# A decode block whose 2560-byte output is stored by two four-row transfers from two engines, in place of one eight-row transfer

## The chip, the cores and the metric

The kernel runs on one core of a Trainium2 chip. The core has a matrix engine (TensorE, PE in the profile), three engines for elementwise work (VectorE or DVE, ScalarE or ACT, GpSimd or POOL), a sequencer without arithmetic that issues transfers (SyncE, SP), and 16 DMA engines that move data between HBM and the on-chip memories. Each engine runs its own list of instructions; they meet through semaphores. The metric is the device time of one execution in microseconds; before the change it is 187.03 us, the median of three runs (186.99 to 187.13).

## The reference

One decode step of a block with adaptive layer norm, for a batch of two rows of 640 numbers in bf16:

```python
mod = (_silu(c) @ w_mod).reshape(c.shape[0], 6, 1, -1)
sa, ca, ga, sb, cb, gb = (mod[:, 0].copy(), ...)
h = _layernorm(x, axis=-1) * (1 + ca) + sa
x = x + ga * _A_ref(h, A_k_cache, A_v_cache, A_wq, A_wo)
h = _layernorm(x, axis=-1) * (1 + cb) + sb
x = x + gb * _B_ref(h, B_w_gate, B_w_up, B_w_down)
return x
```

`_A_ref` is attention with 32 heads of 192 numbers over the last 1024 positions of the two caches, and `_B_ref` is a feed-forward part with 1536 hidden numbers and a gelu gate. The result is 2 x 1 x 640 numbers, 2560 bytes.

## The kernel before, in words

Some 77 MB of caches and weights stream in from HBM, in transfers that SyncE issues in a fixed order: the modulation weights, the two small inputs, the query weights, four K tiles, five V tiles, the output projection, and last the gate, up and down weights of the feed-forward part. The large tiles share a ring of four slots and the space of the query weights, so SyncE waits for an earlier tile's last reader before it issues the load of the next tile.

The rows of the batch are not kept as two long rows. A row of 640 numbers is folded into `NJ = 4` pieces of 160, and piece j of batch row b lies on partition 32 j + 16 b of a 128 x 160 tile. So the eight pieces sit on partitions 0, 16, 32, ... 112 (`rows_of`, L277), and in HBM they are reached by a view of two outer dimensions, four pieces by two batch rows (`dram_rows`, L280). The inputs `c` and `x` come in by this pair of views (L328, L329), and the output leaves by it (L680).

The scores are made on VectorE (products at L465) and summed by TensorE and VectorE (L476, L483); after the softmax the values are summed on TensorE (L523). After the output projection (L628) the second layer norm, the gate and up products (L646), gelu (L653), and the down product (L669) follow each other closely, each with its weights landing shortly ahead. The last two elementwise operations, on VectorE, multiply the down product by the modulation (L676) and add the residual into the tile `sc` (L678).

A small scheduler of the kernel's own (`_Sched`, L28) keeps one list of operations for each engine, in the order in which the program names them. `S.op` adds a computation, `S.dma` a transfer with a semaphore of its own; both work out from the named reads and writes which operations must come first, and `emit` (L79) writes the lists out with a wait ahead of an instruction whose semaphore has not been waited for yet (L93). A transfer's wait is usually folded into the transfer's own instruction at L274. The output transfer is the last entry of SyncE's list; it waits for L678. After it SyncE waits until the transfer has landed (L683), and nothing else stands on any engine. ScalarE's list ends with gelu (L653).

Of the kernel before, what the change touches and what calls it, by code (L numbers as in the profile page):

```python
# [103 lines left out]
def bass_adaLN_cond__sliding_block_cached__geglu_ffn__decode_kernel(  # L104
# [15 lines left out]
    P = 128  # L120
# [5 lines left out]
    SQ = 32  # L126
    NJ = P // SQ
    BS = SQ // 2
# [43 lines left out]
    with es:  # L172
        S = _Sched(nc, es)
# [48 lines left out]
        sc = sb("sc", [P, DN], BF16)  # L222
# [36 lines left out]
        def bank(k):  # L259
            return ("bank", k)  # L260
# [7 lines left out]
        sem_wu = [S.sem("d_wu%d" % i) for i in range(len(WU_SPLIT))]  # L268
        sem_wd = [S.sem("d_wd%d" % i) for i in range(len(WD_SPLIT))]
        sem_ring = [S.sem("d_ring%d" % i) for i in range(4)]  # L270
        sem_out = S.sem("d_out")

        def k_dma(dst, src):
            return lambda e: e.dma_start(dst, src)  # L274


        def rows_of(tile):  # L277
            return tile[0:P:BS, :]

        def dram_rows(v):  # L280
            return v.rearrange("b (j n) -> j b n", j=NJ)
# [8 lines left out]
             reads=[("S", 0, 0, 0), ("S", 0, 0, 1), ("S", 0, 1, 0), ("S", 0, 1, 1)], writes=["ident_f"], name="ident_f")  # L290
        S.op("pool", lambda e: e.tensor_copy(out=ident_b[:, :], in_=ident_f[:, :]),
             reads=["ident_f"], writes=["ident_b"], name="ident_b")
# [3 lines left out]
             reads=["ident_f"], writes=["G32"], name="G32")  # L296
        S.op("dve", lambda e: e.tensor_reduce(out=M32[:, :], in_=ident_f[:, :].rearrange("p (h t) -> p h t", t=QP), axis=AX.X, op=ALU.add),
             reads=["ident_f"], writes=["M32"], name="M32")
# [3 lines left out]
             reads=["G32"], writes=["Bsel"], name="Bsel")  # L302
# [3 lines left out]
             reads=["M32"], writes=["DS"], name="DS")  # L306


        for b in range(2):
            S.op("dve", (lambda b: lambda e: e.tensor_copy(  # L310
                out=SEL[:, b, :, BS * b:P:SQ], in_=G32[:, :].rearrange("p (j m) -> p m j", m=HM)))(b),
                reads=["G32"], writes=["SEL"], name="SEL%d" % b)
        for b in range(2):
            for m in range(HM):
                S.op("dve", (lambda b, m: lambda e: e.tensor_copy(
                    out=Qsel[:, b, m, :].rearrange("p (a m t) -> p a m t", a=NJ, m=HM)[:, :, m, :],
                    in_=ident_f[:, BS * b:P:SQ].unsqueeze(2).broadcast_to([P, NJ, QP])))(b, m),
                    reads=["ident_f"], writes=["Qsel"], name="Qsel%d%d" % (b, m))
# [277 lines left out]
        for i, nt in enumerate(OT_SPLIT):  # L596
            S.op("dve", (lambda t0, nt: lambda e: e.transpose(oT[:, t0:t0 + nt, :], oc.rearrange("p (q k) -> p k q", k=NT)[:, t0:t0 + nt, :]))(t0, nt),
                 reads=[("oc", c) for c in range(NQC)], writes=[("oT", t) for t in range(t0, t0 + nt)], name="oT%d" % i)
# [24 lines left out]
        for i, (ta, tb) in enumerate(wo_of):  # L623
            def f(e, ta=ta, tb=tb):
# [10 lines left out]
             reads=[bank(BK_M), ("modC", 0)], writes=[("lnt", 0)], name="ga_attn")  # L635
        S.op("dve", lambda e: e.tensor_tensor(out=X2[:, 0, :], in0=lnt[:, 0, :], in1=X2[:, 0, :], op=ALU.add),
             reads=[("lnt", 0)], writes=[("X2", 0)], name="x1")
# [3 lines left out]
        def ffn_gu(bk, wv, key, name, ka, kb):  # L641
            def f(e):
# [11 lines left out]
             reads=[bank(BK_G[0])], writes=["gl"], name="gelu")  # L654
        k0 = 0
        for ci, nk in enumerate(WU_SPLIT):
# [4 lines left out]
             reads=[bank(BK_G[1]), "gl"], writes=["aC"], name="geglu")  # L661
        to_contraction(aT[:, :, :], aC[:, :], FT, ["aC"], ["aT"], "aT")
        f0 = 0
        for ci, nf in enumerate(WD_SPLIT):
            def f(e, f0=f0, nf=nf):
# [11 lines left out]
             reads=[bank(BK_C), ("modC", 1)], writes=[("lnt", 1)], name="gb_y")  # L677
        S.op("dve", lambda e: e.tensor_tensor(out=sc[:, :], in0=lnt[:, 1, :], in1=X2[:, 0, :], op=ALU.add),  # L678
             reads=[("lnt", 1), ("X2", 0)], writes=["sc"], name="outC")
        S.dma("sp", k_dma(dram_rows(out[:, 0, :]), rows_of(sc)), sem_out, reads=["sc"], name="st_out")  # L680

        S.emit("sp", nc.sync)
        nc.sync.wait_ge(sem_out, 16)  # L683
        S.emit("pool", nc.gpsimd)
        S.emit("act", nc.scalar)
        S.emit("dve", nc.vector)
# [29 lines left out]
```

## Time and profile before

| what | value |
|---|---|
| median of the runs | 187.03 us (186.99 to 187.13) |
| span of the profiled execution, from its first to its last instruction | 185.7 us |
| mean granted TensorE clock | 0.915 |
| TensorE matmul / VectorE / ScalarE busy | 63% / 57% / 7% of the span |
| read from HBM | 76.88 MB, 414 GB/s over the span |
| issue of the output transfer on SyncE | starts at 183.93 us, lasts 0.635 us |
| SyncE's wait for it to land (L683) | 1.1 us |

The profile gives for the profiled execution its span only; the run times stand 1.3 us above it (187.03 against 185.7), which is what lies around the first and the last instruction. In the lines of the profile a number with L is a line of the kernel, SPq and ACTq are the lists of instructions that SyncE and ScalarE step through, and DMA_DIRECT2D is the instruction that issues a transfer: its duration is the time that the issuing engine spends on it, not the time in which the bytes move. A share such as 57% is an average over stages with different limits; for the change at hand only the last few microseconds matter.

### The profile page before, as it was taken

Reading aid. Unit: us, or ns where it says so; the run is one execution under the profiler, and the core shown is the slowest. Engines: PE = TensorE matmul, PEld = TensorE weight load, DVE = VectorE, ACT = ScalarE, POOL = GpSimd, SP = SyncE. Lnnn points to the kernel's source line nnn. Section 1 sums busy time; section 2 is a strip of 40 time slices with the busy share of each in tenths; the row PEclk is TensorE's granted clock in tenths of the full one; section 3 lists DMA queues with packets and bytes.
Section 4 is the critical chain, followed back from the end, with each engine's and each line's share of the span. In section 5 each row is a group of like instructions: output and inputs, shape, how many; then the busy total and the mean of one; then the engine's idle time right before and its main releaser. Section 6 shows DMA issues by size and latency. Waiting matters only on the chain.

```text
span 185.7 us, 2254 instructions
## 1 busy us (share of the span) xinstructions
PE 117.2 (63%) x1014; PEld 60.8 (33%) x1014; DVE 106.6 (57%) x114; ACT 13.9 (7%) x24; POOL 4.9 (3%) x12
## 2 busy tenths in 40 slices
PE   0004500871079899988999885349928977299844
PEld 0001200440024334433344342226614654265422
DVE  6801600020598999999999993294556714803331
ACT  2001400013000000000000000200010004100400
POOL 8200000000000000000000000000000000000000
PEclk9999999998559999999999999558996999859999
DMA  7999998898999989899999989899999999999991
GB/s 248 414 437 477 463 463 389 371 491 371 487 413 434 468 381 459 381 487 402 455 424 434 459 381 466 381 487 413 395 434 424 424 435 424 413 408 435 422 392 50
DMA packets 2925, 77.02 MB, mean 415 GB/s; under 512 B 356, under 2 KB 356, under 8 KB 868
## 3 DMA queue, kind: packets, MB, share of 16 engines
q1 hardware_dynamic: 2916, 76.88, 96.7%
q8 instruction: 8, 0.13, 0.3%
q14 instruction: 1, 0.01, 0.0%
HBM read 76.88 MB, written 0.00 MB: 414 GB/s over the span
## 4 chain that ended last, share of the span: by engine, by line
DMA 43%; DVE 36%; PE 16%; SPq 1%; ACT 1%; issue 1%; POOL 1%; DVEq 0%; POOLq 0%
DMA ring<-in_A_k_cache_dram 24%; DVE ring L465 19%; DMA ring<-in_B_w_down_dram 18%; PE ps L523 10%; DVE r L465 7%; DVE Sg L483 5%; PE ps L476 4%; DVE Em L511 2%; SPq L274 1%; ACT E_sb L502 1%; PE ps L504 1%; PE ps L498 1%; DVE On L540 0%; ACT On L536 0%; PE ps L491 0%
## 5 line engine op out<-in xcount | busy, mean ns | idle before, releaser
L465 DVE TENSOR_TENSOR ring<-ring,qbc 128x6144 bf16<-128x6144 bf16 x12 | 40.1, 3351 | 8.4 <-DMA ring<-in_A_k_cache_dram 8.4
L476 PE MATMUL ps<-ring,ident_b 128*128 128x512 bf16 x144 | 34.7, 393 | 13.0 <-DVE ring L465 13.0
L454 PE MATMUL ps<-qbc,ident_b 128*128 128x384 bf16 x120 | 24.7, 339 | 0.7 <-ACT qbc L432 0.7
L523 PE MATMUL ps<-ring,Em 128*64 128x384 bf16 x192 | 19.6, 371 | 7.8 <-DVE Em L511 6.6
L476 PEld LDWEIGHTS ps<-ring,ident_b 128*128 128x128 bf16 x144 | 13.6, 100 | 32.7 <-DVE ring L465 17.2
L511 DVE TENSOR_TENSOR Em<-E_sb,M32b 128x2048 bf16<-128x2048 bf16 x8 | 18.1, 2288 | 5.5 <-PE ps L523 5.5
L523 PEld LDWEIGHTS ps<-ring,Em 128*64 128x64 bf16 x192 | 12.4, 125 | 14.6 <-DVE Em L511 7.3
L454 PEld LDWEIGHTS ps<-qbc,ident_b 128*128 128x128 bf16 x120 | 11.6, 101 | 10.9 <-issue 2.8
L401 PE MATMUL ps<-ring,scT 128*32 128x480 bf16 x40 | 4.4, 601 | 16.0 <-DVE scT L358 16.0
L465 DVE TENSOR_TENSOR r<-r,qbc 128x6144 bf16<-128x6144 bf16 x4 | 13.4, 3352 | 0.0
L483 DVE TENSOR_REDUCE Sg<-ps 128x32 f32<-128x512 f32 x16 | 11.0, 687 | 3.4 <-PE ps L476 3.4
L424 PE MATMUL ps<-r,hT 128*32 128x384 bf16 x80 | 5.8, 475 | 10.7 <-DMA r<-in_A_wq_dram 10.7
L476 PE MATMUL ps<-r,ident_b 128*128 128x512 bf16 x48 | 11.1, 380 | 1.8 <-DVE r L465 1.8
L434 DVE CAST aux<-ps 128x384 bf16<-128x384 f32 x4 | 2.0, 553 | 16.6 <-PE ps L424 15.7
L628 PE MATMUL ps<-r,aux 128*32 128x160 bf16 x192 | 5.1, 271 | 4.4 <-DMA r<-in_A_wo_dram 2.6
L424 PEld LDWEIGHTS ps<-r,hT 128*32 128x32 bf16 x80 | 3.2, 135 | 13.8 <-issue 11.6
L476 PEld LDWEIGHTS ps<-r,ident_b 128*128 128x128 bf16 x48 | 4.4, 98 | 8.1 <-DVE r L465 3.4
L401 PEld LDWEIGHTS ps<-ring,scT 128*32 128x32 bf16 x40 | 1.2, 132 | 17.5 <-DVE scT L358 16.0
L540 DVE TENSOR_SCALAR On<-ps,rden 32x192 bf16<-32x192 f32 x4 | 1.7, 418 | 8.9 <-ACT On L536 8.9
L502 ACT ACTIVATE E_sb<-Sg,nb 128x256 bf16<-128x256 f32 x2 | 1.0, 507 | 75.6 <-DVE nb L501 75.6
L628 PEld LDWEIGHTS ps<-r,aux 128*32 128x32 bf16 x192 | 4.3, 114 | 5.8 <-DMA r<-in_A_wo_dram 3.6
L523 PE MATMUL ps<-r,Em 128*64 128x384 bf16 x64 | 5.4, 327 | 0.0
(73 smaller groups left out, 65.6 us busy)
## 6 DMA issues: line engine op xcount, KB each, us to landing
ring<-in_A_k_cache_dram SPq DMA_DIRECT2D x3, 6144.0 KB, 40.3
ring<-in_A_v_cache_dram SPq DMA_DIRECT2D x2, 6144.0 KB, 23.3
r<-in_A_wq_dram SPq DMA_DIRECT2D x1, 7680.0 KB, 30.7
r<-in_A_k_cache_dram SPq DMA_DIRECT2D x1, 6144.0 KB, 38.4
r<-in_A_v_cache_dram SPq DMA_DIRECT2D x1, 6144.0 KB, 23.3
ring<-in_A_v_cache_dram SPq DMA_DIRECT2D x2, 3072.0 KB, 17.6
r<-in_A_wo_dram SPq DMA_DIRECT2D x2, 2560.0 KB, 23.7
ring<-in_w_mod_dram SPq DMA_DIRECT2D x1, 4800.0 KB, 14.2
```

Of the source, the lines that this page charges most:

```text
L274: return lambda e: e.dma_start(dst, src)
L401: last = e.matmul(ps[SQ * j:SQ * j + SQ, bk, 0:3 * DN].rearrange("p (i n) -> p i n", i=3), lhsT=scT[:, k, :], rhs=wm_v[:, k, 3 * part * D: ...
L424: last = e.matmul(ps[SQ * j:SQ * j + SQ, BK_H + c, 0:QC], lhsT=hT[:, k, :], rhs=wq_v[:, k, RN * j + QC * c:RN * j + QC * (c + 1)], start=( ...
L434: S.op("dve", lambda e: e.tensor_copy(out=dst, in_=src), reads=reads, writes=writes, name=name)
L454: last = e.matmul(ps[:, bk, 0:2 * Dh], lhsT=ident_b[:, :], rhs=qbc[:, :, :].rearrange("p b d -> p (b d)"), start=True, stop=True)
L465: S.op("dve", lambda e: e.tensor_tensor(out=tile_v(ks)[:, hf * JH:(hf + 1) * JH, :], in0=tile_v(ks)[:, hf * JH:(hf + 1) * JH, :], in1=qbc[ ...
L476: last = e.matmul(o_ap, lhsT=ident_b[:, :], rhs=tile_v(ks)[:, hf * JH:(hf + 1) * JH, ci * GC:(ci + 1) * GC], start=(ci == 0), stop=(ci == ...
L483: S.op("dve", lambda e: e.tensor_reduce(out=S_sb[:, b, a:a + JH], in_=ps[:, hf, 0:JH * GC].rearrange("p (j c) -> p j c", j=JH), axis=AX.X, ...
L502: S.op("act", lambda e: e.activation(out=E_sb[:, b, :], in_=S_sb[:, b, :], func=ACTF.Exp, scale=SCALE, bias=nb[:, 0:1], accum_out=esum[:, ...
L511: S.op("dve", lambda e: e.tensor_tensor(out=Em[:, t % 2, :, :], in0=E_sb[:, b, J * t:J * (t + 1)].unsqueeze(2).broadcast_to([P, J, H]), in ...
L523: last = e.matmul(ps[r:r + 2 * H, BK_O, 0:ON], lhsT=Em[:, t % 2, 2 * jp:2 * jp + 2, :].rearrange("p j c -> p (j c)"), rhs=tile_v(vs)[:, 2 ...
L628: last = e.matmul(ps[SQ * j:SQ * j + SQ, BK_M, 0:DN], lhsT=oT[:, t, :], rhs=wo_v[:, t, DN * j:DN * j + DN], start=(t == 0), stop=(t == NT ...
```

## The change

The one store of eight rows becomes two stores of four rows. Batch row 0 (partitions 0, 32, 64, 96 of `sc`) is issued by SyncE, batch row 1 (partitions 16, 48, 80, 112) by ScalarE. Each has a semaphore of its own, both wait for L678, and SyncE waits for the two semaphores at the end, one after the other. The view in HBM of each store has one outer dimension of four pieces that follow each other without a gap, where the view before had two. In the order of instructions, SyncE's list keeps its length with the last transfer of the new form; ScalarE's list grows by one transfer at its end; TensorE's, VectorE's and GpSimd's lists are the same.

```diff
-        sem_out = S.sem("d_out")
+        sem_out = [S.sem("d_out%d" % b) for b in range(2)]
...
-        S.dma("sp", k_dma(dram_rows(out[:, 0, :]), rows_of(sc)), sem_out, reads=["sc"], name="st_out")
+        for b, eng in enumerate(("sp", "act")):
+            S.dma(eng, k_dma(out[b, 0, :].rearrange("(j n) -> j n", j=NJ), sc[BS * b:P:SQ, :]), sem_out[b], reads=["sc"], name="st_out%d" % b)

         S.emit("sp", nc.sync)
-        nc.sync.wait_ge(sem_out, 16)
+        for s_out in sem_out:
+            nc.sync.wait_ge(s_out, 16)
```

## The prediction

> **What bounds the kernel now.** I read the chain that ended last first: for 185.7 us it goes through loads, VectorE's products and TensorE's sums, and the change touches none of these. So only the stretch behind the last sum matters, and I read it in the timeline, from the last matmul to the end:
>
> ```profile
> 182.85 0.32 PE L669 MATMUL ps<-ring,aux 128*32 128x160 bf16 x8
> 183.22 0.32 DVE L676 TENSOR_TENSOR lnt<-ps,modC 128x160 f32<-128x160 f32 x1 [2.48 <-PE ps L669]
> 183.58 0.32 DVE L678 TENSOR_TENSOR sc<-lnt,X 128x160 bf16<-128x160 f32 x1
> 183.93 0.64 SPq L274 DMA_DIRECT2D out_dram<-sc  x1
> ```
>
> The columns are start, duration, engine, line. VectorE finishes the output tile just ahead of 183.93, SyncE then spends 0.64 us on issuing the store, to 184.57. What follows is in SyncE's own list of waits:
>
> ```profile
> SPq L274 <- DVE sc L678: 32.7, 1, 32.7
> SPq L683 <- DMA out_dram<-sc: 1.1, 1, 1.1
> ```
>
> SyncE had been waiting 32.7 us for the tile, so it starts the issue at once; and after the issue it waits 1.1 us for the landing. 183.93 + 0.64 + 1.1 = 185.67, the end of the span. Nothing else is on the chip in that time, as the table of stretches shows, cut at the end of the issue:
>
> ```profile
> 184.57:185.19 0.62, 0.00 (x0) 0.00 (x0) 0.00 (x0) 0.00 (x0) 0.00 (x0) 0.80 0.00 0
> 185.19:185.31 0.12, 0.00 (x0) 0.00 (x0) 0.00 (x0) 0.00 (x0) 0.00 (x0) 0.50 0.10 21
> 185.31:185.67 0.36, 0.00 (x0) 0.00 (x0) 0.00 (x0) 0.00 (x0) 0.00 (x0) 0.50 0.00 0
> ```
>
> After the stretch and its length come the five engines' busy time, the clock, the DMA engines' busy share and GB/s. For 0.62 us after the issue no byte moves, the eight rows move within 0.12 us at a share of 0.10, and 0.36 us later the landing is seen. So the tail of 1.74 us is 0.64 issue, 0.62 until the first packet, 0.12 of packets, 0.36 until SyncE goes on. The issue depends most visibly on the form of the transfer; here are SyncE's issues by form, with the least, median and greatest ns:
>
> ```profile
> L274 SPq DMA_DIRECT2D ring<-in_A_v_cache_dram x4: 535/535/535, 82.6 to 130.6; - x4
> L274 SPq DMA_DIRECT2D r<-in_A_wo_dram x4: 343/432/432, 135.8 to 137.2; - x4
> ...
> L274 SPq DMA_DIRECT2D ring<-in_w_mod_dram x1: 373/373/373, 0.8 to 0.8; - x1
> L274 SPq DMA_DIRECT2D cc<-in_c_dram x1: 692/692/692, 1.2 to 1.2; - x1
> L274 SPq DMA_DIRECT2D xc<-in_A_x_dram x1: 547/547/547, 2.0 to 2.0; - x1
> ...
> L274 SPq DMA_DIRECT2D ring<-in_B_w_gate_dram x1: 328/328/328, 147.1 to 147.1; - x1
> L274 SPq DMA_DIRECT2D ring<-in_B_w_up_dram x1: 434/434/434, 147.5 to 147.5; - x1
> L274 SPq DMA_DIRECT2D out_dram<-sc x1: 635/635/635, 183.9 to 183.9; - x1
> ```
>
> The cache tiles have a view with two outer dimensions in HBM (heads by position groups) and cost 535 when SyncE comes out of a wait. The weights have one outer dimension: 328 to 343 out of a wait (the gate weights, the first of the four output projection parts), 432 to 434 when another issue stands right ahead (the other parts, the up weights). The eight-row transfers cost 547 to 692.
>
> **The change part by part.** The sum is made on the profiled execution, whose span of 185.67 us is all that the profile gives of it; 1.3 us lie around that up to the median of 187.03, and I take these as unchanged and apply the difference to the median.
>
> *The store's form, on SyncE.* Removed: one issue of two outer dimensions, 635. Added: one of one outer dimension, four rows. No row shows that form at four rows. Going from two outer dimensions to one is worth 535 - 335 = 200 ns among issues out of a wait, so I take 635 - 200 = 435. The ends are 328, the cheapest issue in the trace, and 635, no gain. That would end SyncE's issue at 183.93 + 0.435 = 184.37, 0.20 us earlier.
>
> *The second store, on ScalarE.* Added: one issue on an engine that issues no transfer before. Its work is done at 175.6 us (gelu starts at 175.14 and lasts 0.49), so it stands waiting for L678 as SyncE does and starts at 183.94; nothing is queued behind it on ScalarE. The trace shows no ScalarE issue, so its price is bounded by SyncE's rows: 328 at the least, at the most 692 for the dearest small issue, or more if it has to queue behind SyncE's. I take 435 as for SyncE, and because both start together I add what an issue pays right behind another, 433 - 328 = 0.105: 0.54 us, to 184.48, against 184.57 before. That is 0.09 us less. This later one of the two sets the end.
>
> *The flight.* 0.62 to the first packet, 0.12, 0.36: taken as before for each store. The rows are eight in all either way, and at a share of 0.10 the 16 DMA engines have room, so two stores side by side cost nothing here; at the worst the second store's packets come after the first's, +0.12 at most, and half the rows for each could take as much as half of 0.12 off.
> The Trainium skill (DMA: Bandwidth & Descriptors, Rules for kernel authors) speaks against the change: two transfers to disjoint partition halves run on the same DMA engines and serialize, so one transfer should be used. By that rule the +0.12 would be paid and the sum would be 187.08; the trace of before holds one store alone and cannot show it.
>
> *The second wait of SyncE, and the new semaphore.* The wait at L683 is one instruction of 17 ns in the trace; a second one behind it adds 0.02 when both transfers have landed, and nothing is queued behind it but the end. I take 0.02; the bounds are 0 and 0.04. ScalarE now ends at 184.48 where it ended at 175.6; whatever follows on it is covered by SyncE, which waits until about 185.6, so it costs nothing while that issue ends before that.
>
> Sum: -0.09 + 0.02 = -0.07 us, 187.03 - 0.07 = 186.96, which I round to 186.95.
>
> **The rivals.** A measurement of this kernel can tell about 0.2% from no change, 0.37 us: below 186.66 or above 187.40.
>
> *Cheaper all along (faster).* Both issues at 328 with no queueing: -0.31 + 0.02, 186.74. To count as faster, another 0.08 must come off the flight, as it would if the 0.62 us between the issue and the first packet were also longer for two outer dimensions than for one: at 0.5 instead of 0.62 the time is 186.62. For it speaks that the 635 is the dearest of all issues out of a wait; against it that no row of an idle queue shows the flight of another form.
>
> *The form saves nothing (same).* Four rows or eight, one dimension or two, 635 each and side by side: 187.03 + 0.02 = 187.05, or the ScalarE issue 0.105 longer, 187.16. The two small loads speak for it, 547 and 692 with the same views: a spread of 145 with no form to explain it.
>
> *One after the other (slower).* If the two issues cannot run at the same time, the second starts when the first is done. At the reduced price the second ends 0.435 + 0.475 (the spacing of two issues of the weights, 147.46 to 147.94) = 0.91 after the start, 0.275 later than before's 0.635: 187.32, still within 0.2%. At the unreduced price it ends at 1.27: +0.635 + 0.02, 187.69. The same time results if ScalarE's first issue alone takes about 1.25 us. It decides from about 1.0 us on: 0.635 + 0.37. For it speaks that an issue behind another is dearer by 0.105 on one engine; against it that 0.105 is far less than a whole issue.
> The Trainium skill (Perfetto Trace Analysis, DMA Instruction — HWDGE) says that the block that generates descriptors is shared by the two issuing sequencers and locked for exclusive use, with the lock wait inside the profiled duration. By that rule one of the two issues would show as longer by up to the other's length; no row of before has two issuers, so only the price between 0.105 and a whole issue is open.
>
> **How the numbers follow.** The sum with its small queueing cost: 0.37, at 186.95, from 186.80 to 187.10. The form saves nothing: 0.10. One after the other at the reduced price: 0.10. One after the other at the full price, or a dear first issue on ScalarE: 0.23. Cheaper all along: 0.20, of which 0.17 below 186.66 and 0.03 between that and 186.74. The rest of the first three cases' spread puts 0.03 more above 187.40. So faster 0.17, same 0.57, slower 0.26. The range reaches down to 186.60 (cheap issues and a flight of 0.5), and up to 187.46: the reduced price in series, 187.32, and the 145 by which the two small loads differ, for a first issue on ScalarE. About 0.04 is left out below and 0.15 above, mostly the full price in series.
>
> **What would show it.** In the profile of after, SyncE's issue should be about 0.44 and ScalarE's about 0.54 us, both starting within 0.02 of each other behind L678; the first packets some 0.6 us after the issue, a DMA share still near 0.1, and SyncE's waits ending about 1.1 us after ScalarE's issue ended. Everything before 183.9 should be as it was. An issue on ScalarE over 1.0 us, or one that starts its packets only after SyncE's have landed, makes the prediction wrong upwards; a stretch without packets shorter than 0.5 us makes it wrong downwards. A change in the loads' stretch would mean that something moved which I took to be untouched.

## The result and the profile after

The changed kernel takes 187.41 us (median of 21 runs, 187.12 to 187.75) against 187.04 us before; the ratio is 1.0018, with a 95% interval of 1.0011 to 1.0024. By that ratio it is 0.34 us slower (0.21 to 0.45), where the prediction had 0.07 faster. Run a second time beside other kernels it came out at 1.0015 (1.0007 to 1.0024). The time lies inside the range; the direction was wrong.

The timeline of the changed kernel's end, with the columns of before:

```profile
182.97 0.32 PE L669 MATMUL ps<-ring,aux 128*32 128x160 bf16 x8
183.35 0.33 DVE L676 TENSOR_TENSOR lnt<-ps,modC 128x160 f32<-128x160 f32 x1 [2.48 <-PE ps L669]
183.71 0.33 DVE L678 TENSOR_TENSOR sc<-lnt,X 128x160 bf16<-128x160 f32 x1
184.06 0.59 SPq L274 DMA_DIRECT2D out_dram<-sc  x1
184.06 1.33 ACTq L274 DMA_DIRECT2D out_dram<-sc  x1
```

Both issues start at 184.06. SyncE's takes 0.59, not the predicted 0.44; ScalarE's takes 1.335 (1.33 in the line above), not 0.54. Where the time goes is clearer in the table of stretches (stretch, length, the engines' busy time, clock, the DMA engines' busy share, GB/s), which I cut at the packets of the two stores:

```profile
184.06:185.29 1.23, 0.00 (x0) 0.00 (x0) 0.00 (x0) 0.00 (x0) 0.00 (x0) 1.00 0.00 0
185.29:185.38 0.09, 0.00 (x0) 0.00 (x0) 0.00 (x0) 0.00 (x0) 0.00 (x0) 1.00 0.08 14
185.38:185.57 0.19, 0.00 (x0) 0.00 (x0) 0.00 (x0) 0.00 (x0) 0.00 (x0) 1.00 0.00 0
185.57:185.66 0.09, 0.00 (x0) 0.00 (x0) 0.00 (x0) 0.00 (x0) 0.00 (x0) 1.00 0.08 14
185.66:186.02 0.36, 0.00 (x0) 0.00 (x0) 0.00 (x0) 0.00 (x0) 0.00 (x0) 1.00 0.00 0
```

SyncE's four rows move 1.23 us after the common start (the packets in the trace: from 185.296), then nothing for 0.19 us, then ScalarE's four rows (from 185.572), 0.28 us behind. The last 0.36 us are as before. So the tail, from the start of the issue to the end of the span, grew from 1.74 to 1.96 us: +0.22. The profiled span is 186.0 us instead of 185.7; the other 0.13 us lie ahead of 184.06, in a stretch that the change does not touch and in which profiles of these kernels differ by more (the first store behind the output tile began between 183.87 and 184.72 us in the runs below). I therefore read the experiments by their tails, and use the times as a check.

SyncE's own waits after the change:

```profile
SPq L274 <- DVE sc L678: 32.5, 1, 32.5
SPq L685 <- DMA out_dram<-sc: 1.3, 1, 1.3
```

The wait for the landing is 1.3 where it was 1.1, although the issue ahead of it is shorter.

### The profile page after: what moved, and what is told of

Read it like the earlier page. It is cut to its first block, busy times and chain, and to the rows that moved or that the text cites. A ratio compares the mean times of both kernels' runs of the same rounds, so it can differ in the third digit from the quotient of the medians.

```text
span 186.0 us, 2255 instructions
## 1 busy us (share of the span) xinstructions
PE 116.6 (63%) x1014; PEld 60.5 (33%) x1014; DVE 106.6 (57%) x114; ACT 13.9 (7%) x24; POOL 4.9 (3%) x12
## 4 chain that ended last, share of the span: by engine, by line
DMA 42%; DVE 36%; PE 17%; SPq 1%; ACT 1%; issue 1%; POOL 1%; DVEq 0%; POOLq 0%
DMA ring<-in_A_k_cache_dram 24%; DVE ring L465 19%; DMA ring<-in_B_w_down_dram 18%; PE ps L523 11%; DVE r L465 7%; DVE Sg L483 5%; PE ps L476 4%; DVE Em L511 2%; SPq L274 1%; ACT E_sb L502 1%; PE ps L504 1%; PE ps L498 1%; DVE On L540 0%; ACT On L536 0%; PE ps L491 0%
## 5 line engine op out<-in xcount | busy, mean ns | idle before, releaser
L476 PE MATMUL ps<-ring,ident_b 128*128 128x512 bf16 x144 | 35.5, 400 | 13.9 <-DVE ring L465 13.9
L454 PE MATMUL ps<-qbc,ident_b 128*128 128x384 bf16 x120 | 23.9, 330 | 0.7 <-ACT qbc L432 0.7
L424 PE MATMUL ps<-r,hT 128*32 128x384 bf16 x80 | 5.0, 422 | 11.0 <-DMA r<-in_A_wq_dram 11.0
```

What stands on the lines that cost most here:

```text
L424: last = e.matmul(ps[SQ * j:SQ * j + SQ, BK_H + c, 0:QC], lhsT=hT[:, k, :], rhs=wq_v[:, k, RN * j + QC * c:RN * j + QC * (c + 1)], start=( ...
L454: last = e.matmul(ps[:, bk, 0:2 * Dh], lhsT=ident_b[:, :], rhs=qbc[:, :, :].rearrange("p b d -> p (b d)"), start=True, stop=True)
L476: last = e.matmul(o_ap, lhsT=ident_b[:, :], rhs=tile_v(ks)[:, hf * JH:(hf + 1) * JH, ci * GC:(ci + 1) * GC], start=(ci == 0), stop=(ci == ...
```

## The experiments

Three theories stood at first. *First issue*: a program's first transfer on ScalarE pays a one-time price. *Queueing*: ScalarE's issue waits for SyncE's. *The engine*: ScalarE always takes 1.3 us for an issue. Below, "start to packet" is the time from the start of a store's issue to its first packet in the trace. In the kernel before it is 1.27 us (183.93 to 185.20). The diffs show the lines that an experiment is about; "..." stands for changes left out, which are the declarations of tiles and semaphores, the wait at the end, and lines that the text names.

**Both stores on SyncE.**

```diff
-        for b, eng in enumerate(("sp", "act")):
+        for b, eng in enumerate(("sp", "sp")):
```

> The two four-row stores are both issued by SyncE, one behind the other; ScalarE issues nothing. Theory 'first issue' (a program's first transfer on ScalarE pays a one-time 0.7 us), theory 'queueing' (ScalarE waits for SyncE's issue) and theory 'the engine' (each issue on ScalarE takes about 1.3 us) agree here on the first issue, 0.59 us as in the changed kernel, if ScalarE's issue beside it did not lengthen it. The second should take 0.43 to 0.6, so that it ends 1.1 to 1.25 us after the start against 0.64 before: 187.5 to 187.65 us. If it ends at or below 187.2, the time is not set by the end of the issue.

Measured: 187.58 us, ratio 1.0031 (1.0020 to 1.0042). The issues take 0.594 and 0.560 us, starting 0.64 apart; each store's first packet stands 1.23 and 1.20 us after its own start, and the tail is 2.29 us, +0.55. The split alone, without ScalarE, costs one issue. With ScalarE it cost 0.22, so the second engine does save something against two stores in one list, but nothing against one store.

**The one store on ScalarE.**

```diff
-        S.dma("sp", k_dma(dram_rows(out[:, 0, :]), rows_of(sc)), sem_out, reads=["sc"], name="st_out")
+        S.dma("act", k_dma(dram_rows(out[:, 0, :]), rows_of(sc)), sem_out, reads=["sc"], name="st_out")
```

> The kernel before with its one store of eight rows issued by ScalarE in place of SyncE. 'First issue' and 'the engine': ScalarE's issue takes 1.3 to 1.4 us with nothing beside it, and the tail from the issue's start to the end of the span is about 1.94 us as in the changed kernel against 1.74 before: 187.2 to 187.4 us. 'Queueing': 0.64 us and 187.0 us.

Measured: 187.05 us, ratio 1.0000 (0.9991 to 1.0009). The issue in the timeline of this kernel, and the stretches behind its start:

```profile
184.72 1.11 ACTq L274 DMA_DIRECT2D out_dram<-sc  x1
```

```profile
184.72:185.98 1.26, 0.00 (x0) 0.00 (x0) 0.00 (x0) 0.00 (x0) 0.00 (x0) 1.00 0.00 0
185.98:186.09 0.11, 0.00 (x0) 0.00 (x0) 0.00 (x0) 0.00 (x0) 0.00 (x0) 1.00 0.11 23
186.09:186.45 0.36, 0.00 (x0) 0.00 (x0) 0.00 (x0) 0.00 (x0) 0.00 (x0) 0.89 0.00 0
```

None of the theories had this. The issue is long without any company (against *queueing*: 1.11 us where SyncE took 0.635), and yet the first packet stands 1.27 us after the start, as from SyncE, the tail is 1.74 us and the time is that of before. (The profiled execution of this kernel is the slowest of its ten, 187.71 us; its excess lies ahead of 184.72.) The extra length of this issue is not on the path: its first packet comes 0.17 us after its end, where SyncE's came 0.63 after the end of a 0.635 us issue.

**ScalarE's store as its second transfer.**

```diff
-        S.dma("sp", k_dma(rows_of(xc), dram_rows(A_x[:, 0, :])), sem_x, writes=["xc"], name="ld_x")
+        S.dma("act", k_dma(rows_of(xc), dram_rows(A_x[:, 0, :])), sem_x, writes=["xc"], name="ld_x")
```

> The changed kernel, with the small load of x at the start issued by ScalarE, so that its store is its second transfer. 'First issue': the load takes about 1.3 us on ScalarE, hidden under the loads, and the store's issue falls to 0.55 to 0.7 us; time 186.95 to 187.1. 'Queueing' and 'the engine': the store's issue stays at 1.3 us, time 187.3 to 187.45.

Measured: 187.19 us, ratio 1.0008 (0.9998 to 1.0017). The load takes ScalarE 1.132 us at the start, the store only 0.563, so the long issue is a matter of the first transfer. But the tail is 1.91 us, +0.17; the time alone would not tell this kernel from before. Now ScalarE's packets come first, 1.21 after the start, and SyncE's are the late ones, 1.48 after theirs. *First issue* is right about the instruction and wrong about the tail.

**Four rows on SyncE, alone.**

```diff
-        sem_out = [S.sem("d_out%d" % b) for b in range(2)]
+        sem_out = [S.sem("d_out0")]
...
-        for b, eng in enumerate(("sp", "act")):
+        for b, eng in enumerate(("sp",)):
```

> SyncE alone stores batch row 0 in the new four-row form; batch row 1 is not stored. It prices the form by itself. If the form is worth the 0.2 us of the prediction, the issue is 0.44 us and the time 186.85. If the 0.592 us of the changed kernel is the form's own price, the issue is 0.59 and the time 186.95 to 187.05: the 0.2 us were wrong whatever ScalarE does. All three theories on ScalarE say the same here, except that 'queueing' with both sides affected would give 0.44.

Measured: 186.99 us, ratio 0.9997 (0.9988 to 1.0006); issue 0.589 us, start to packet 1.23, tail 1.67. The four-row form by itself saves 0.05 of the issue, 0.04 of the way to the first packet and 0.07 of the tail, not 0.2.

From here on the theory was *sharing*: a store's first packet comes about 1.23 us after the start of its issue whatever the issue's length, and of two stores issued together the second is held up by about 0.26 us more. The runs bear out the second half; the first half does not hold, as the next section shows.

**The second store 8 us ahead.** (In the runs of this kind "st_out1" reads the tile of the input x and stands in place of ScalarE's store at the end; SyncE keeps its four-row store.)

```diff
              reads=[bank(BK_G[0])], writes=["gl"], name="gelu")
+        S.dma("act", k_dma(out[1, 0, :].rearrange("(j n) -> j n", j=NJ), xc[BS:P:SQ, :]), sem_out[1], reads=["xc"], name="st_out1")
...
```

> The changed kernel, but batch row 1's store takes its data from the input x, not from the result, and is issued by ScalarE right behind gelu at 175.6 us, 8 us ahead of SyncE's. Both transfers are kept, their coincidence is gone. Theory 'sharing' (each store needs about 1.23 us from the start of its issue to its first packet, and when both are issued together the second is held up by a further 0.26 in something that both issuers share; the length of the issue does not count): SyncE's store as when alone, first packet 1.23 after its start, tail 1.65 us, 186.95 to 187.05. If the changed kernel's loss comes from something that a second transfer costs at any time (the end of the program, another queue), the time stays at 187.3 to 187.45.

Measured: 186.92 us, ratio 0.9993 (0.9984 to 1.0003); ScalarE's store began 8.8 us ahead, at 175.22; SyncE's issue 0.592, start to packet 1.23, tail 1.66. With two transfers, two semaphores and two waits, but not at the same moment, the loss is gone. The second queue and the second wait cost nothing measurable.

**The second store 0.30 us ahead.**

```diff
              reads=[bank(BK_C), ("modC", 1)], writes=[("lnt", 1)], name="gb_y")
+        S.dma("act", k_dma(out[1, 0, :].rearrange("(j n) -> j n", j=NJ), xc[BS:P:SQ, :]), sem_out[1], reads=["xc", ("lnt", 1)], name="st_out1")
...
```

> As the run with row 1's data from x, but ScalarE's store is issued 0.36 us ahead of SyncE's: it waits for the multiplication ahead of the last addition. 'Sharing' with 0.26 us a store: ScalarE's store has passed when SyncE's comes, so SyncE's first packet stands 1.23 after its start again, 187.0. If instead an issuer holds the other off for the whole length of its issue (1.1 to 1.3 us on ScalarE the first time, 0.6 later), SyncE's first packet comes 0.25 to 0.95 later, at 1.5 to 2.2 after its start, and the time is 187.25 to 187.95.

Measured: 187.05 us, ratio 1.0000 (0.9991 to 1.0009). ScalarE's issue runs from 183.94 for 1.09 us, SyncE's from 184.25 for 0.59, wholly inside it; SyncE's start to packet is 1.23. One issuer does not hold the other off for the length of its issue. 0.30 us of distance is enough.

**The changed kernel again, and with a late small load to warm ScalarE's queue.**

```diff
+        S.dma("act", k_dma(rows_of(spare), dram_rows(A_x[:, 0, :])), sem_spare, writes=["spare"], name="ld_spare")
...
+        nc.sync.wait_ge(sem_spare, 16)
         for s_out in sem_out:
```

> The changed kernel once more, to stand beside the next run on the same chip: 187.3 to 187.45; ScalarE's issue 1.3 us.

> The changed kernel with one small load of x into an unused tile issued by ScalarE behind gelu at 175.6 us, so that ScalarE's store at the end is its second transfer, with everything ahead of 175 as it was. 'Sharing': ScalarE's issue is 0.56 to 0.6 in place of 1.3, yet the time is the changed kernel's within 0.1 us (187.25 to 187.45), since the later of the two stores still comes 0.26 late. Theory 'cold' (the length of ScalarE's first issue costs time at the end): 0.2 us less than the changed kernel or more, 187.0 to 187.2.

Measured: 187.28 us, ratio 1.0015 (1.0007 to 1.0024) for the changed kernel, and 187.56 us, ratio 1.0028 (1.0018 to 1.0038) with the load. The stores of the latter in its timeline:

```profile
184.07 0.59 SPq L276 DMA_DIRECT2D out_dram<-sc  x1
184.08 0.55 ACTq L276 DMA_DIRECT2D out_dram<-sc  x1
```

ScalarE's issue has fallen from 1.33 to 0.55 us and the kernel has not become faster. That is against *cold*. The kernel became slower than *sharing* expected, by 0.11 beyond its upper end: the gap between the two first packets is 0.35 here (SyncE's 1.55 after its start), and SyncE ends with one wait instruction more behind the last landing, 0.07 us in the trace. The spread of the gap from 0.26 to 0.35 is not explained.

**GpSimd as the second issuer.**

```diff
-        for b, eng in enumerate(("sp", "act")):
+        for b, eng in enumerate(("sp", "pool")):
```

> The two four-row stores, batch row 0 by SyncE as in the changed kernel, batch row 1 by GpSimd in place of ScalarE, both waiting for the last addition. It asks what SyncE and ScalarE share. If it is something on the side of the DMA engines (two transfers at once on the same engines, from whatever issuer), one of the two first packets stands 0.26 to 0.35 us behind the other again, or SyncE's moves to 1.5 after its start. If it is something that only these two issuers share, SyncE's first packet stands at 1.23 after its start as alone. GpSimd's own store has no row so far; I expect 1.0 to 2.5 us to its first packet, and the time between 186.9 and 188.2 goes by that alone.

Measured: 187.32 us, ratio 1.0011 (1.0002 to 1.0020). SyncE's start to packet is 1.24, GpSimd's 1.26 (from 184.15 to 185.41), but GpSimd starts 0.27 us after SyncE, so by the run with 0.30 us between the stores the two had hardly an occasion to collide. Of the 0.32 us by which the tail grew, 0.27 are GpSimd's late start. The question stayed open.

**A wide load beside the store.**

```diff
         S.dma("sp", k_dma(dram_rows(out[:, 0, :]), rows_of(sc)), sem_out, reads=["sc"], name="st_out")
+        S.dma("act", k_dma(wide[:, :], B_w_down[0:P, 0:DN]), sem_wide, reads=["sc"], writes=["wide"], name="ld_wide")
...
```

(Left out with the rest: a small load by ScalarE behind gelu, so that this one is its second transfer.)

> The kernel before, its eight-row store on SyncE, with two loads on ScalarE that nothing uses: a small one behind gelu at 175.6 us (so that the next is not ScalarE's first), and at the end, beside the store, one of 128 rows of 320 bytes. It asks whether the hold-up grows with the size of the other transfer. A fixed price for a transfer: one of the two first packets 0.26 to 0.35 us behind the other, SyncE's first packet at 1.27 or at about 1.55 after its start, time 187.3 to 187.6. A price by rows (0.26 for four rows, 32 times as many here): SyncE's first packet 2 us later or more if ScalarE's load goes first, 189 or more; if SyncE's goes first, ScalarE's first packet still only 0.3 to 0.6 behind.

Measured: 187.06 us, ratio 0.9997 (0.9987 to 1.0006), a miss for the 187.3 to 187.6 expected of a fixed price and far from the 189 of a price by rows. In the timeline:

```profile
184.06 0.63 SPq L278 DMA_DIRECT2D out_dram<-sc  x1
184.07 0.35 ACTq L278 DMA_DIRECT2D wide<-in_B_w_down_dram  x1
```

The issue of 128 rows takes 0.35 us, less than that of four, and its first packet comes 0.98 us after its start where a store of four rows from ScalarE needed 1.21. SyncE's first packet then came at 1.26, unharmed: the two were 0.28 us apart anyhow. Beside the load's rows the store landed later, though, the last row 1.86 us after the start of the issue against 1.70 before, and the tail is 1.91; the time, at most 0.11 us slower by its interval, does not show that.

**Eight rows in one dimension, and a store behind a recent load.**

```diff
-        S.dma("sp", k_dma(dram_rows(out[:, 0, :]), rows_of(sc)), sem_out, reads=["sc"], name="st_out")
+        S.dma("sp", k_dma(out.rearrange("b o (j n) -> (b o j) n", j=NJ), rows_of(sc)), sem_out, reads=["sc"], name="st_out")
```

> The kernel before with its one store of eight rows by SyncE, written to HBM one row behind the other in the order of the partitions, so that the view has one outer dimension; the pieces of the result stand in another order than the reference's. If the number of outer dimensions set the issue's price as the prediction took it (0.2 us), the issue is 0.44; by the four-row store alone it is 0.59 to 0.6. In either case the first packet stands about 1.23 to 1.27 us after the start, and the time is 186.95 to 187.05.

```diff
         to_contraction(aT[:, :, :], aC[:, :], FT, ["aC"], ["aT"], "aT")
+        S.dma("sp", k_dma(rows_of(spare), dram_rows(A_x[:, 0, :])), sem_spare, reads=["aT"], writes=["spare"], name="ld_spare")
...
```

> The kernel before with one more small load of x by SyncE into an unused tile, issued behind the transpose at 180.8 us, so that SyncE has issued nothing for 3 us instead of 33 us when the store comes. If the 1.23 us from the start to the first packet is partly the price of a queue that stood idle, the first packet comes earlier, by 0.1 us or more, and the time falls below 186.95. If it is fixed, the time is 187.0 to 187.15.

Measured: 187.06 us, ratio 0.9999 (0.9990 to 1.0009), with an issue of 0.666 us in one dimension against 0.635 in two; and 187.10 us, ratio 1.0000 (0.9990 to 1.0010), start to packet 1.24. The number of dimensions is not what makes the store's issue dear, and SyncE's 33 us without an issue are not what makes the packets late.

Three runs were meant to settle what the two stores share. **GpSimd released earlier:**

```diff
              reads=[bank(BK_C), ("modC", 1)], writes=[("lnt", 1)], name="gb_y")
+        S.dma("pool", k_dma(out[1, 0, :].rearrange("(j n) -> j n", j=NJ), xc[BS:P:SQ, :]), sem_out[1], reads=["xc", ("lnt", 1)], name="st_out1")
...
```

> Batch row 0 by SyncE from the result, batch row 1 from the input x by GpSimd, which is released by the multiplication ahead of the last addition, so that it starts about 0.08 us ahead of SyncE and the two come to the DMA engines together (SyncE alone: first packet 1.23 after its start; GpSimd: 1.26 after its own). If the hold-up arises on the DMA engines' side, one of the two first packets is 0.25 us or more later than that. If only SyncE and ScalarE hold each other up, both keep 1.23 and 1.26 within 0.05, and the time is 186.95 to 187.1.

Measured: 187.35 us, ratio 1.0011 (1.0002 to 1.0021). GpSimd's issue again began 0.24 us after SyncE's (184.44 against 184.20), although it had been released 0.35 ahead; first packets 1.23 and 1.25 after their starts. The two did not meet, and whether GpSimd was itself held up before its recorded start can't be told. Inconclusive.

**ScalarE 0.07 us ahead:**

```diff
+        S.op("act", lambda e: e.activation(out=tiny[:, 1:2], in_=lnt[:, 1, 0:1], func=ACTF.Copy), reads=[("lnt", 1)], writes=["tiny"], name="tiny")
+        S.dma("act", k_dma(out[1, 0, :].rearrange("(j n) -> j n", j=NJ), xc[BS:P:SQ, :]), sem_out[1], reads=["xc", "tiny"], name="st_out1")
...
```

> Row 1 from x by ScalarE again, now about 0.05 to 0.1 us ahead of SyncE's store instead of 0.30: a one-element operation on ScalarE stands between the multiplication and its store. If each store holds something for about 0.26 us, one of the two first packets is late by 0.15 to 0.3 us against 1.23 after its own start. If only starts within a few ns of each other collide, neither is.

Measured: 187.24 us, ratio 1.0008 (0.9997 to 1.0020), in the stretches from the start of ScalarE's issue:

```profile
184.02:185.26 1.24, 0.00 (x0) 0.00 (x0) 0.04 (x1) 0.00 (x0) 0.00 (x0) 1.00 0.00 0
185.26:185.35 0.09, 0.00 (x0) 0.00 (x0) 0.00 (x0) 0.00 (x0) 0.00 (x0) 1.00 0.10 14
185.35:185.53 0.18, 0.00 (x0) 0.00 (x0) 0.00 (x0) 0.00 (x0) 0.00 (x0) 1.00 0.00 0
185.53:185.62 0.09, 0.00 (x0) 0.00 (x0) 0.00 (x0) 0.00 (x0) 0.00 (x0) 1.00 0.08 14
```

ScalarE's packets come 1.24 after its start, undisturbed; SyncE's at 185.53, 1.45 after its start at 184.08, so 0.22 late. The gap is 0.27 again, with the starts 0.07 apart: a store holds something for about 0.27 us, and the next one waits for the rest of it.

**A wide load held back to meet the store:**

```diff
+        S.op("act", lambda e: e.activation(out=tiny[:, 1:2], in_=sc[:, 0:1], func=ACTF.Copy), reads=["sc"], writes=["tiny"], name="tiny")
+        S.dma("act", k_dma(wide[:, :], B_w_down[0:P, 0:DN]), sem_wide, reads=["sc", "tiny"], writes=["wide"], name="ld_wide")
...
```

> The eight-row store on SyncE and the 128-row load on ScalarE as before, but the load held back by about 0.25 us, so that the first packets of the two, 1.27 and 0.98 after their starts when undisturbed, would come at the same moment. If a wide transfer holds the shared thing as a narrow one does, one of the two first packets is 0.15 us or more later than that. If only two narrow transfers collide, neither is.

Measured: 187.47 us, ratio 1.0022 (1.0012 to 1.0032), where the end now waits for the load's landing. The load's first packet is at 0.98 after its start, as before; the store's at 1.38, 0.11 late and 0.16 behind the load's first. That is between the two answers expected. The load's 128 rows also occupy the DMA engines themselves (by an estimate from packets of some 20 ns in the trace, eight rows on each engine if they are dealt out evenly, 0.16 us), so this run does not separate the two places.

**Two rows against four:**

```diff
+        S.dma("act", k_dma(out[1, 0, 0:2 * DN].rearrange("(j n) -> j n", j=2), xc[BS:P // 2:SQ, :]), sem_out[1], reads=["xc", "tiny"], name="st_out1")
...
```

> As act_bit_ahead, but ScalarE's store, 0.07 us ahead, has two rows of x instead of four (the other two pieces of batch row 1 are not stored). If the work of a store is dealt out by rows over the DMA engines, one row to each, two of SyncE's four rows meet ScalarE's and two do not. If the hold-up arises at the DMA engines, SyncE's four first packets split: two about 1.23 us after SyncE's start, two about 1.45. If it arises ahead of them, in something that hands out a whole transfer, all four come late by about 0.2 us together, or, if its length goes by rows, by about 0.1.

Measured: 187.18 us, ratio 1.0003 (0.9991 to 1.0014). The stretches:

```profile
183.97:185.19 1.22, 0.00 (x0) 0.00 (x0) 0.03 (x1) 0.00 (x0) 0.00 (x0) 1.00 0.00 0
185.19:185.25 0.06, 0.00 (x0) 0.00 (x0) 0.00 (x0) 0.00 (x0) 0.00 (x0) 1.00 0.07 11
185.25:185.46 0.21, 0.00 (x0) 0.00 (x0) 0.00 (x0) 0.00 (x0) 0.00 (x0) 1.00 0.00 0
185.46:185.56 0.10, 0.00 (x0) 0.00 (x0) 0.00 (x0) 0.00 (x0) 0.00 (x0) 1.00 0.07 13
```

After ScalarE's two rows no packet moves for 0.21 us, and then all four of SyncE's come together, the first 1.44 after its start (184.03), 0.27 behind ScalarE's first, as with four rows. So the hold-up does not arise from rows that meet at a DMA engine, and between two and four rows its length goes by the transfer and not by its rows. That a row goes to an engine of its own is an assumption of this reading; the semaphores speak for it, with four landings seen for four rows and two for two.

The trace has a second sign that needs no such assumption. The semaphore of each store from SyncE is updated once ahead of any of its packets. In the six runs in which SyncE and ScalarE issued small stores within 0.07 us of each other, that update stands 0.60 to 0.74 us behind the end of SyncE's issue, in all others 0.41 to 0.42. In the changed kernel it is late (0.60) before a packet of either store has moved, so the two issuers meet in something ahead of the packets. It is not the packets' own delay: SyncE's packets are on time there.

## Why the prediction was wrong

*What bounds the end.* Right: nothing but the tail changed, and the tail was read correctly into issue, gap, packets, landing.

*The flight: 0.62 us from the end of the issue to the first packet.* Right for every issue that nothing held up, but for one kind. The stretches from the end of the issue to the first packet, for four rows on SyncE alone, eight rows in one dimension on SyncE, the wide load on ScalarE, and the eight rows that ScalarE issued as its first transfer:

```profile
184.46:185.09 0.63, 0.00 (x0) 0.00 (x0) 0.00 (x0) 0.00 (x0) 0.00 (x0) 1.00 0.00 0
184.73:185.36 0.63, 0.00 (x0) 0.00 (x0) 0.00 (x0) 0.00 (x0) 0.00 (x0) 1.00 0.00 0
184.42:185.05 0.63, 0.00 (x0) 0.00 (x0) 0.00 (x0) 0.00 (x0) 0.00 (x0) 1.00 0.00 0
185.82:185.98 0.16, 0.00 (x0) 0.00 (x0) 0.00 (x0) 0.00 (x0) 0.00 (x0) 1.00 0.00 0
```

With the packets of the trace, where nothing held the transfer up:

| transfer | issue, us | end of the issue to first packet, us |
|---|---|---|
| 128 rows, ScalarE's second | 0.35 | 0.64 |
| four rows, ScalarE's second | 0.55 | 0.65 |
| four rows, SyncE | 0.59 | 0.64 |
| eight rows, SyncE, the kernel before | 0.635 | 0.63 |
| eight rows in one dimension, SyncE | 0.67 | 0.635 |
| four rows, ScalarE's first | 1.07 to 1.09 | 0.16 |
| eight rows, ScalarE's first | 1.11 | 0.17 |

So a shorter issue does bring the first packet forward by as much, as the prediction had it, and the first half of *sharing* is wrong: the "1.23 us whatever the length" holds only because the small stores' issues lie so close together, with the wide load at 0.98 and the longest of SyncE's at 1.30. Only the extra half microsecond of ScalarE's first issue is not on the path. The prediction held against its rival "cheaper all along" that no row of an idle queue shows the flight of another form; the trace of before has one, the first load of the program, with an issue of 0.373 us and its first packet 0.63 us after that.

*The store's form on SyncE, 435 ns.* Wrong in size. The issue took 0.59 us, so 0.04 came off and not 0.20, and the first packet came 0.04 earlier. The 200 ns between two dimensions and one were read from transfers of 128 rows and carried over to four; eight rows in one dimension took 0.666. The four-row store's true gain, measured alone, is 0.07 us of the tail.

*The second store on ScalarE, 0.54 us.* The issue took 1.335, the first transfer on that engine; as a second transfer it took 0.55 to 0.56, close to the predicted 0.54. By the prediction's path, 1.335 in place of 0.635 would have given 187.75, and its sign of an error upwards, an issue over 1.0 us, was met. None of the extra length reached the end: 1.11 us alone cost nothing, and 0.55 in place of 1.33 gained nothing. That two errors cancelled here, a first issue about 0.5 us longer than SyncE's and a gap behind it 0.48 shorter, is luck.

*Two stores side by side cost nothing, +0.12 at the worst.* This is the step that failed and turned the sign. The second store's packets are 0.26 to 0.35 us behind the first's when both are issued together, although the DMA engines stand at a share of 0.08. The rival "one after the other" came nearest, since it lets one store wait for the other, but at the wrong size: it set a whole issue (0.475 to 0.635 us) where about 0.27 us are held, and its ends of 187.32 and 187.69 stand on both sides of the measured 187.41. By the corrected sum: 0.59 + 0.64 + 0.27 in place of 0.635 + 0.63 to the later first packet, +0.23, against a tail that grew by 0.22 and a time that grew by 0.34 (0.21 to 0.45). The time lies inside the range because the range had been drawn up to 187.46 for two rivals, not because its own sum held.

*The second wait, 0.02.* Small, as predicted, in the changed kernel: the span ends 0.045 us behind the last landing there against 0.033 before. In the changed kernel with the late small load on ScalarE, where a wait for a store that had already landed came last, that wait added 0.07, above the bound of 0.04.

*The rules weighed.* The Trainium skill (DMA: Bandwidth & Descriptors, Rules for kernel authors) said that two transfers to disjoint partition halves serialize and one should be used. It was right in direction. Its ground, that both share the same DMA engines, is not what the trace shows: the two-row run, with the assumption named there, puts the hold-up ahead of the engines, and the late semaphore updates point the same way. The Trainium skill (Perfetto Trace Analysis, DMA Instruction — HWDGE) has a block that makes the descriptors, shared by the two issuers and locked for one at a time. The 0.27 us by the transfer would agree with that, if only a part of the issue holds it. It also says that the lock wait lies inside the profiled duration; here the rows are divided. Where ScalarE's first store was the late one, its issue took 1.335 us against 1.07 to 1.13 otherwise, which fits. Where SyncE's store was the late one, in four runs, its issue took 0.592 to 0.602 us against 0.589 to 0.592 undisturbed, which does not. That the block named there is what holds the stores is not shown: with GpSimd as a second issuer the two never met.

## What to carry to other kernels

Read the end of a kernel from the issue of its last store: here the issue, then 0.63 to 0.65 us to the first packet, then about 0.1 of packets and 0.36 to the end. The length of the issue counts, so compare it among transfers of the same number of rows before you carry a price over. The exception in these runs is ScalarE's first transfer, whose recorded issue ends 0.16 us ahead of the packets: its extra length is no loss at the end. Splitting a short store over two issuers at the same moment makes the later half late by about 0.27 us here; half the rows gave back only 0.07. Where two small transfers must leave near the end, start them 0.3 us apart if one of them can be ready earlier. No variant tried beat the kernel before by more than its interval.

## What the runs showed that was not expected

- The first transfer that ScalarE issues in a program takes 1.07 to 1.13 us of the engine when it is alone or ahead of SyncE's, and took 1.335 both times that SyncE's was 4 ns ahead; the second takes 0.55 to 0.56, or 0.35 for 128 rows. At the end of the program the extra length costs nothing (1.11 us alone, ratio 1.0000). Whether an instruction close behind it on ScalarE is delayed by it was not measured.
- A small transfer is dearer to issue than a wide one: 0.55 to 0.67 us for four or eight rows, 0.33 to 0.35 for 128 rows in one dimension, out of a wait. The wide one's first packet also came earlier, 0.98 us after the start against 1.2 to 1.3. A last store of 128 rows was not run.
- It is open what the two issuers share, and why the gap between two small stores was 0.35 us in one run and 0.26 to 0.28 in the others.
